# Loads in paced halves and quarters, and a new order at both ends of attention, in a one-core attention and expert-routing kernel

## The chip, the cores and the metric

The kernel runs on one core of a Trainium2 chip. The metric is the time of one execution on the device, in microseconds (us), as the median of several runs. A profile is one further execution, with its own time; its span runs from the first to the last instruction of the program.

## What is computed

Eight batches of eight heads, 576 tokens, 64 features a head, all in float32. For each head the product of k transposed and v (64 by 64) is applied to q, and each token's 64 outputs are normalised by their root mean square. The 4608 tokens, each now 512 wide, then go through one of eight experts, the one whose logit is largest.

```python
kv = np.einsum('bhsd,bhse->bhde', k, v)
out = np.einsum('bhsd,bhde->bhse', q, kv)
rms = np.sqrt(np.mean(out * out, axis=-1, keepdims=True) + 1e-06)
x = out / rms * g_norm                      # (B, S, H * D) -> (4608, 512)
logits = x @ w_gate                         # (4608, 8)
expert_idx = np.argmax(logits, axis=1)
gate_w = softmax(logits)[expert_idx]
for e in range(8):                          # D = 512, F = 1024
    h = np.maximum(x[mask_e] @ w1[e], 0.0)
    out[mask_e] = gate_w[mask_e, None] * (h @ w2[e])
```

## The kernel before

**Two stages.** Attention runs over 36 slots of 128 tokens, and sends each token's normalised row, in float16, to a table in HBM (`xs_scratch`) with a part for each expert. Then the experts run one after the other: each fetches 608 rows of its part through a transposing DMA, multiplies them with w1 (`block`, L680), applies relu on ScalarE, multiplies with w2 (`two`, L704) and scatters the gated result to the output. Rows over 608 go to a left-over job and a loop that is seldom entered.

**Order.** The order on every engine is written out by hand (`manual_schedule`, L773); each engine runs its own instructions in program order and waits for the others through semaphores. A slot `s` of the loop at L901 issues, in this order: `x_mm(s)`, q times kv with the gate's columns attached, into the PSUM tile `op` (two buffers); what the list `mid` holds for this slot; `x_qt(s + 2)`, the transposes of q on TensorE, into `qtp` (one buffer); `x_norm(s)`, the squares on ScalarE and their sum on VectorE; the list `pre`; `x_qs(s + 2)`, ScalarE's copy of the transposed q; `x_qp(s + 3)`, GpSimd's reordering copy of the loaded q; the list `late`; `rest()`, which is Ln and Exp on ScalarE, the scaled gate columns (`lr`, L354) and the scaled rows (`xh`, L359) on VectorE; and the list `last`.

The lists carry the products of k and v of the next batch (`kv_mm`, four pieces a batch, into the tile `kvp`), the copy from `kvp` (`kv_copy`), the transposes of kv and their copy (`kv_t`, `kv_tcopy`), the product with the gate weights (`kv_gate`, `kv_gcopy`), and the steps of routing a group of 2 to 5 slots (`Route`): logits, largest logit, choice, running counts, ranks on TensorE (`ranks`, L430), row numbers, and one scatter a slot on GpSimd (`scatter`, L464). `early_count` and `early_close` fix how many rows of expert 0 lie below 384 before the last groups are routed, so that its first 384 rows can be fetched, and multiplied with w1 (`early_pair`, L696), while the last slots are still routed. `zeros` issues matmuls on a tile of zeros.

**Loads.** SyncE issues all large loads in program order, on one hardware queue that is spread over 16 DMA engines. A load of k, v or q of one batch is 1152 KB, of one weight matrix 2048 KB, each one DMA (L204, L156, L162); only k and v of batch 0 come in two halves. They land in ten places of `land`, and the first five weight loads go into places of `land` that attention has left. `blank_rows` (L218) writes 128 rows a expert of a zero row with gate sum 1 into `xs_scratch`. `load_next` issues the next weight load.

Of the kernel before, what the change touches and what calls it, by code (L numbers as in the profile page):

```python
# [28 lines left out]
def kernel(  # L29
# [11 lines left out]
    nc = tc.nc  # L41
# [54 lines left out]
    c_f16 = nc.inline_tensor(c16, name="c_f16")  # L96

# [50 lines left out]

    class Weights:
# [4 lines left out]
        def load1(self, buf, eng):  # L154
            self.s1 = buf.rearrange("p (t f) -> p t f", t=4)
            eng.dma_start(  # L156
                self.s1, moe_w1[self.e, :, :].rearrange("o (t p) f -> p (o t) f", p=128)
            )

        def load2(self, buf, eng):  # L160
            self.s2 = buf.rearrange("p (t d) -> p t d", t=8)
            eng.dma_start(  # L162
                buf.rearrange("p (t c) -> p t c", t=4),
                moe_w2[self.e, :, :].rearrange("o (t p r) d -> p (o t) (r d)", p=128, r=2),
            )
# [22 lines left out]
    def load_next(count=1):  # L188
        nonlocal n_loads
        for _ in range(count):  # L190
            if n_loads < len(loads):
                n, m = loads[n_loads]
                (W[n].load1 if m == 1 else W[n].load2)(stg[n_loads % 5], nc.sync)
                n_loads += 1
# [3 lines left out]
    def load(name, b, parts=1):  # L198
        src = {"k": k, "v": v, "q": q}[name]
        n = {"k": (2 * b) % 6, "v": (2 * b + 1) % 6, "q": 6 + b % 4}[name]  # L200
        ld[name, b] = land[:, n, :].rearrange("p (i c) -> p i c", i=4)
        view = src[b].rearrange("(i hh) (p j) d -> (hh p) i (j d)", hh=2, j=9)
        return [
            lambda ii=slice(4 // parts * m, 4 // parts * (m + 1)): nc.sync.dma_start(  # L204
                ld[name, b][:, ii, :], view[:, ii, :]
            )
            for m in range(parts)
        ]
# [9 lines left out]
    def blank_rows():  # L218
        nc.sync.dma_start(
            xs.ap().rearrange("(e s) c -> s e c", e=E)[CAP - 128:CAP, :, :],  # L220
            _bc(blank, 1, E),
        )
        nc.sync.dma_start(
            xs.ap().rearrange("(e s) c -> s e c", e=E)[CAP:CAP + 32, :, 256:258],
            _bc(blank[0:32, 256:258], 1, E),
        )
# [87 lines left out]

    def x_mm(s):
        P, r, b = split(s)
        if r < 8:
            parts = [(slice(0, 128), kvs_bufs[b % 4])]
        else:
            parts = [(HALF[tok], kvs_bufs[(2 * P + tok) % 4]) for tok in range(2)]  # L320
        ops[s] = PSA.tile([128, 4, 256], F32, tag="op", bufs=2, name="op")
        for i4 in range(4):
            for cols, kvs in parts:
                nc.tensor.matmul(  # L324
                    ops[s][cols, i4, 0:144], qts[s][:, i4, cols], kvs[:, i4, :],
                    start=True, stop=True,
                )

    def x_norm(s):
# [18 lines left out]
        def rest():  # L348
# [9 lines left out]
            )  # L358
            nc.vector.tensor_tensor(  # L359
# [3 lines left out]
            )  # L363
        return rest
# [4 lines left out]
    class Route:  # L369
# [60 lines left out]
        def ranks(self, s=None):  # L430
            G = self.G
            if s is None:
                self.pp = PSA.tile([128, G, 8], F32, tag="misc", bufs=1, name="pp")
            else:
                self.pp = ops[s][:, 0, 144:144 + 8 * G].rearrange("p (t e) -> p t e", e=8)
# [182 lines left out]
    class Job:  # L618
# [84 lines left out]

        def two(self, t, yp=None):  # L704
# [69 lines left out]
    with tc.tile_pool(name="psattn", bufs=1, space=bass.MemoryType.PSUM) as PSA:  # L774
        first_slot = [9 * (b // 2) + 4 * (b % 2) for b in range(B)]
        mid, pre, late, last = ({s: [] for s in range(-4, 40)} for _ in range(4))
# [4 lines left out]
        for b in range(1, B):  # L781
            f = first_slot[b]
            for m, piece in enumerate(KV_PIECES):
                at(late, 1 + m // 2 if b == 1 else f - 5 + (m + 1) // 2 if b < 4 else f - 6 + m,
                   kv_mm, b, *piece)
            at(last, f - 2 if b == 1 else f - 3, kv_copy, b)
            at(mid, f - 1 if b == 1 else f - 2, kv_t, b)
            at(pre, f - 1 if b == 1 else f - 2, kv_tcopy, b)
            at(late if b == 1 else mid, f - 1, kv_gate, b)
            at(late if b == 1 else pre, f - 1, kv_gcopy, b)  # L790
# [5 lines left out]
            ((2, 0, 5), (23, 24, 25, 26), (26, 27, 28, 29, 29)),  # L796
            ((2, 5, 4), (27, 28, 29, 30), (30, 30, 31, 31)),
            ((3, 0, 4), (31, 32, 32, 33), (33, 33, 34, 34)),
        ]
        for g, (s_sum, s_below, s_oh, s_rank), s_scat in plan:  # L800
            rt, G = Route(*g), g[2]
            at(late, s_sum, rt.logits, 0, G)
            at(late, s_below - (s_below == s_oh), rt.top)
# [6 lines left out]
            at(mid, s_rank, rt.ranks, s_rank)  # L810
# [12 lines left out]
        at(last, 25, load_next, 1)  # L823
        at(last, 29, load_next, 1)
        ecp = []
        at(mid, 31, lambda: ecp.append(early_count()))
        at(late, 31, lambda: early_close(ecp[0]))
        at(last, 31, jobs[0].fetch, 0, NE)
        at(last, 32, load_next, 1)
        for m, slot in enumerate((31, 32, 33, 34, 34)):  # L830
            at(last, slot, W[0].cast1_act, m)
# [3 lines left out]
        at(late, 34, rt.below)  # L835
        at(late, 34, rt.code)

# [26 lines left out]
        def zeros(count, tag="misc", bufs=1):  # L864
            warm = PSA.tile([128, 4, 256], F32, tag=tag, bufs=bufs, name="warm") \
                if tag == "op" else PSA.tile([128, 2, 256], F32, tag=tag, bufs=bufs, name="warm")
            warm = warm[:, 0:2, :].rearrange("p a c -> p (a c)")

            def more(count):
                for n in range(count):  # L870
                    nc.tensor.matmul(
                        warm, blank[:, 0:64].bitcast(F16), blank[:, 0:256].bitcast(F16),
                        start=True, stop=True,
                    )
            more(count)
            return more
# [15 lines left out]
        more(1)  # L892
        kv_gate(0)
        kv_gcopy(0)
        x_qt(0)
        x_qs(0)
        x_qt(1)
        x_qs(1)
        at(late, 0, zeros, 4)

        for s in range(35):  # L901
# [3 lines left out]
            if s + 2 < 36:  # L905
                x_qt(s + 2)
# [3 lines left out]
            if s + 2 < 36:  # L910
                x_qs(s + 2)
            if s + 3 < 36:
                x_qp(s + 3)
            for fn in late[s]:
                fn()
            rest()
# [7 lines left out]
        relu = [job.early_pair(0, "kvp", 1)]  # L924
        rt.first()
        rt.choose()
        rt.tally()
        rt.ranks()
        relu.append(job.early_pair(2, "op", 2))
        W[0].cast1_act(5)  # L930
        rt.expo()
# [3 lines left out]
        rest()  # L935
        relu[0]()
        W[0].cast1_act(6)
        rt.total()
# [5 lines left out]
        W[0].cast1_act(7)  # L944
# [4 lines left out]
        relu[1]()  # L949
        end.ranks()  # L950
# [4 lines left out]
        W[0].cast2(0)  # L955
        job.early_pair(4, "kvp", 1)()
# [3 lines left out]
        job.early_pair(6, "op", 2)()  # L960
        for t in range(1, 4):
            W[0].cast2(t, nc.vector)
# [6 lines left out]
        W[1].cast1(3)  # L969
        W[1].cast2(3)  # L970

# [3 lines left out]
    if True:  # L975
        jobs[1].fetch()
        load_next(2)
        jobs[0].place(NE, CT)

        for n in range(len(order)):  # L980
# [11 lines left out]
            spans = job.spans if n > 0 else [(EARLY, CAP)]  # L992
# [71 lines left out]
```

## Time and profile before

| what | value |
|---|---|
| time, median of 3 runs | 271.45 us (271.18 to 273.37) |
| time of the profiled execution | 271.81 us, span 269.9 us |
| granted TensorE clock, mean | 0.982 |
| PE busy | 242.6 us (90% of the span) |
| ACT, DVE, POOL busy | 158.6, 142.6, 107.0 us |
| DMA | 82.93 MB, mean 307 GB/s |
| x_mm(0), x_mm(4), x_mm(35) start | 18.68, 32.91, 117.07 us |
| expert 0's first matmul, the second expert's first | 118.95, 141.37 us |

PE is TensorE, PEld its weight loads, DVE is VectorE, ACT ScalarE, POOL GpSimd, SP SyncE. In a timeline a row gives the start in us, the length in us, the engine, the line of the kernel, the operation, what it writes and reads, how many instructions it stands for, and in brackets how long the engine was idle before and what ended that. "issue" is a wait that no semaphore in the profile ended.

### The profile page before, as it was taken

What the parts mean: (1) busy time and instruction counts of PE and PEld (TensorE: products, weight loads), DVE (VectorE), ACT (ScalarE), POOL (GpSimd) and SP (SyncE); (2) the same over time, 40 slices, a digit from 0 to 9 for tenths busy, and PEclk for the clock granted to TensorE, in tenths of its full rate; (3) what the DMA queues carried; (4) which work ended last, traced back from release to release, by engine and by line L of the source; (5) the groups of instructions that cost most, each with busy time, mean ns of one, the idle gap of its engine ahead of it and who ended that gap; (6) DMA issues with size and microseconds to landing.
All of it is one profiled execution on the core that took longest, in us unless ns stands there. A gap on an engine that the chain in (4) does not pass through costs nothing. (4 is left out here: it accounts for less than half of the span.)

```text
span 269.9 us, 6884 instructions
## 1 busy us (share of the span) xinstructions
PE 242.6 (90%) x2705; PEld 171.3 (63%) x2705; DVE 142.6 (53%) x373; ACT 158.6 (59%) x363; POOL 107.0 (40%) x138
## 2 busy tenths in 40 slices
PE   4879699998999978657799999989999999999992
PEld 1658688887888867544377566465574755747740
DVE  0004367787687757987838990462524525333031
ACT  1046567676677658787547738369285692854800
POOL 8032221487278364756521061511504415042142
PEclk9789999999999999999999999999999999999997
DMA  7999999999999999579499999999999999942023
GB/s 231 340 390 393 389 352 336 392 398 400 396 383 404 417 407 352 227 174 351 106 229 410 274 307 417 256 401 359 329 419 321 369 329 313 292 126 100 16 79 109
DMA packets 53010, 82.93 MB, mean 307 GB/s; under 512 B 27747, under 2 KB 29027, under 8 KB 52976
## 3 DMA queue, kind: packets, MB, share of 16 engines
q1 hardware_dynamic: 47472, 67.95, 75.9%
q0 software_dynamic: 5056, 14.26, 14.2%
q10 hardware_dynamic: 448, 0.26, 0.6%
q8 instruction: 22, 0.36, 0.5%
q14 instruction: 12, 0.10, 0.1%
HBM read 62.31 MB, written 16.04 MB: 290 GB/s over the span
## 5 line engine op out<-in xcount | busy, mean ns | idle before, releaser
L694 ACT ACTIVATE xh<-hp 128x304 f16<-128x304 f32 (+2 forms) x128 | 52.2, 411 | 49.6 <-PE hp L682 39.9
L717 POOL DMA_INDIRECT out_dram<-ys,idx x41 | 40.9, 999 | 95.2 <-DVE ys L714 86.3
L709 PE MATMUL yp<-w2b,xh 128*128 128x512 f16 (+1 forms) x304 | 67.1, 379 | 0.0
L682 PE MATMUL hp<-xt,w1b 128*128 128x304 f16 (+2 forms) x512 | 64.4, 286 | 2.1 <-DMA xt<-xs_scratch 2.1
L682 PEld LDWEIGHTS <-w1b 128*128 128x128 f16 x544 | 51.5, 98 | 20.5 <-DMA xt<-xs_scratch 1.7
L714 DVE TENSOR_SCALAR ys<-yp,gate 128x512 f32<-128x512 f32 (+1 forms) x38 | 28.2, 749 | 67.8 <-PE yp L709 67.8
L709 PEld LDWEIGHTS <-xh 128*128 128x128 f16 (+1 forms) x328 | 33.6, 103 | 36.4 <-issue 1.2
L324 PE MATMUL op<-kvs,qts 128*128 128x144 f32 (+1 forms) x320 | 45.2, 300 | 2.6 <-DVE xh L359 1.6
L467 POOL DMA_INDIRECT xs_scratch<-xh,sli x36 | 35.8, 995 | 27.5 <-DVE xh L459 10.4
L324 PEld LDWEIGHTS op<-kvs,qts 128*128 128x128 f32 (+1 forms) x320 | 37.9, 183 | 5.7 <-ACT w1b L174 1.4
L346 DVE TENSOR_REDUCE ms<-sq 128x8 f32<-128x512 f32 x36 | 24.7, 685 | 28.9 <-ACT sq L342 28.4
L342 ACT ACTIVATE sq<-op 128x512 f32<-128x512 f32 x36 | 21.5, 596 | 20.6 <-PE op L324 14.1
L239 PE MATMUL kvp<-land 64*64 64x64 f32 x1152 | 24.7, 229 | 6.4 <-issue 3.4
L297 POOL COPY qp<-land 128x512 f32<-128x512 f32 x32 | 19.5, 616 | 24.1 <-DMA land<-in_q_dram 14.4
L239 PEld LDWEIGHTS kvp<-land 64*64 64x64 f32 x1152 | 20.6, 139 | 12.0 <-issue 12.0
L179 ACT CAST w2b<-land 128x1024 f16<-128x1024 f32 x29 | 28.1, 1042 | 0.0
L359 DVE TENSOR_TENSOR xh<-op,rinv 128x512 f16<-128x512 f32 x36 | 24.5, 679 | 0.0
L307 PE MATMUL qtp<-cf,qp 128*128 128x128 f32 x144 | 22.7, 282 | 1.7 <-POOL qp L297 1.7
L313 ACT COPY qts<-qtp 128x512 f32<-128x512 f32 x36 | 21.0, 584 | 2.2 <-PE qtp L307 1.9
L168 DVE TENSOR_SCALAR w1b<-land,g 128x1024 f16<-128x1024 f32 x28 | 19.6, 753 | 0.0
L307 PEld LDWEIGHTS qtp<-cf,qp 128*128 128x128 f32 x144 | 17.3, 146 | 2.1 <-POOL qp L297 1.1
L350 ACT ACTIVATE lnt<-ms,epsb 128x8 f32<-128x8 f32 x36 | 10.8, 300 | 6.1 <-DVE ms L346 6.0
(129 smaller groups left out, 151.3 us busy)
## 6 DMA issues: line engine op xcount, KB each, us to landing
land<-in_moe_w_dram SPq DMA_DIRECT2D x16, 2048.0 KB, 11.7
land<-in_q_dram SPq DMA_DIRECT2D x8, 1152.0 KB, 15.3
land<-in_k_dram SPq DMA_DIRECT2D x7, 1152.0 KB, 15.0
land<-in_v_dram SPq DMA_DIRECT2D x7, 1152.0 KB, 17.7
land<-in_k_dram SPq DMA_DIRECT2D x2, 576.0 KB, 6.5
land<-in_v_dram SPq DMA_DIRECT2D x2, 576.0 KB
xs_scratch<-blank SPq DMA_DIRECT2D x1, 1032.0 KB, 17.0
out_dram<-ys,idx POOLq DMA_INDIRECT x41, 6.2
```

What stands on the lines that cost most here:

```text
L179: nc.scalar.copy(self.w2[:, part, :], self.s2[:, part, :])
L239: nc.tensor.matmul(kvst[b][HALF[ipar], hh, Dh * ip:Dh * ip + Dh], kb[HALF[hh], i, cols], vb[HALF[hh], i, cols], start=(j == 0), stop=(j == 8),
L307: nc.tensor.transpose(qtps[s][:, ip, :, tok, :], qps[s][:, tok, 2 * ip:2 * ip + 2, :], ident)
L324: nc.tensor.matmul(ops[s][cols, i4, 0:144], qts[s][:, i4, cols], kvs[:, i4, :], start=True, stop=True,)
L346: nc.vector.reduce_sum(ms, sq, axis=AXX)
L359: nc.vector.tensor_tensor(xg[:, r, 0:512].rearrange("p (i c n) -> p c i n", i=2, c=4), oc[:, :, 0:128].rearrange("p c (i n) -> p c i n", i=2),
L467: go = nc.gpsimd.indirect_dma_start(out=xs_views[9 * self.P + g0 + t], out_offset=IndirectOffsetOnAxis(ap=self.sli[:, t:t + 1], axis=0), i ...
L682: nc.tensor.matmul(hp, self.w.w1[:, 2 * (kk % 2) + kk // 2, f // 2 * 256:f // 2 * 256 + 256] .rearrange("p (m r) -> p r m", r=2)[:, f % 2, :],
L694: nc.scalar.activation(self.ht[:, f, c0:c1], hp, ACTF.Relu)
L709: nc.tensor.matmul(yp[0:m, :], self.ht[:, f, t * 128:t * 128 + m], self.w.w2[:, f, :], start=(f == 0), stop=(f == 7),)
L714: nc.vector.tensor_scalar(ys[0:m, :], yp[0:m, :], self.gate[0:m, t:t + 1], None, op0=ALU.mult)
L717: nc.gpsimd.indirect_dma_start(out=self.views[t], out_offset=IndirectOffsetOnAxis(ap=self.idx[0:m, t:t + 1], axis=0), in_=ys[0:m, :], in_o ...
```

## The change

- Every load of q, k and v is now two DMAs of 576 KB, and each of the first five weight loads is four of 512 KB. Each of them is passed to `paced`, which counts 32 descriptors a load and DMA engine and makes the DMA wait on the landing of an earlier one, so that at most 48 are under way. Later weight loads are whole and not paced.
- The blank rows are copied from a constant in HBM, four rows to a piece, and not from a tile in SBUF.
- At the start, `x_qt(0)` and `x_qs(0)` come before `kv_gate(0)`; `more(1)` and the four `zeros` of slot 0 are gone. The last two pieces of `kv_mm(1)` move to `mid` of slot 2, its copy follows there, and its transposes and gate product go into slot 3 between `x_qt(4)` and `x_qt(5)`, which are both issued there.
- For batches 2 to 7, `kv_t` and `kv_tcopy` move from `mid` and `pre` to a new list `head`, behind `x_qs` and `x_qp`.
- `rest` is split: from slot 31 on, the Ln, Exp, `lr` and rows of a slot are issued in the next slot (`held`). Slots 32 and 35 use the tile `kvp` in the place of `op`.
- The routing of the groups (2,5,4) and (3,0,4) moves one slot earlier, `early_count`, `early_close` and the fetch of expert 0's first rows from slot 31 to 30; the choice of the group (3,4,3) moves from behind `x_mm(35)` into slot 34.
- Casts of the first expert's weights: of w1 on ScalarE from slot 29 on, one a slot, and of w2 on VectorE in slots 29 and 30. Two `zeros` are added in each of the slots 31 to 34.
- Behind slot 34 the early products of expert 0 begin with two single ones in the tiles `qtp` and `misc`; the steps of the last two groups are interleaved anew; and expert 0's remaining columns (384 to 608) are multiplied in pairs (`late_pair`) with one relu a pair, still in attention's PSUM pool.

```diff
+    zr = np.zeros((32, 4, RW // 2), np.float32)
+    zr[:, :, RW // 2 - 1] = 1.0
+    c_zero = nc.inline_tensor(zr.reshape(32, 2 * RW).view(np.int32), name="c_zero")
...
+    sent, PACE = [], 48
+
+    def paced(did, count):
+        room = PACE - count
+        for name, n in reversed(sent):
+            room -= n
+            if room < 0:
+                tc.add_manual_dep(
+                    did.ins, name,
+                    mybir.DependencyInfo(
+                        mybir.DependencyClass.Sync, mybir.DependencyReason.DATA
+                    ),
+                    reason="few descriptors wait in the queues at a time",
+                )
+                break
+        sent.append((did.ins.name, count))
...
-        def load1(self, buf, eng):
+        def load1(self, buf, eng, parts=1):
...
+            for m in range(parts):
+                t = slice(4 // parts * m, 4 // parts * (m + 1))
+                did = eng.dma_start(self.s1[:, t, :], view[:, t, :])
+                if parts > 1:
+                    paced(did, 32 // parts)
...
-    def load(name, b, parts=1):
+    def load(name, b, parts=2):
...
-            xs.ap().rearrange("(e s) c -> s e c", e=E)[CAP - 128:CAP, :, :],
-            _bc(blank, 1, E),
+            xs.ap().rearrange("(e s) c -> e s c", e=E)[:, CAP - 128:CAP, :].rearrange(
+                "e (p r) c -> e p (r c)", r=4
+            ),
+            _bc(c_zero.ap(), 0, E),
...
-        ops[s] = PSA.tile([128, 4, 256], F32, tag="op", bufs=2, name="op")
+        ops[s] = quad("kvp" if s in (32, 35) else "op", "op")
...
+        def late_pair(self, f, tag):
...
+            for n in range(2):
+                self.block(hp[:, n, 0:CAP - EARLY], f + n, EARLY, CAP)
+            nc.scalar.activation(
+                self.ht[:, f:f + 2, EARLY:CAP], hp[:, :, 0:CAP - EARLY], ACTF.Relu,
+            )
...
-            at(mid, f - 1 if b == 1 else f - 2, kv_t, b)
-            at(pre, f - 1 if b == 1 else f - 2, kv_tcopy, b)
-            at(late if b == 1 else mid, f - 1, kv_gate, b)
-            at(late if b == 1 else pre, f - 1, kv_gcopy, b)
+            at(head, f - 2, kv_t, b)
+            at(head, f - 2, kv_tcopy, b)
+            at(mid, f - 1, kv_gate, b)
+            at(pre, f - 1, kv_gcopy, b)
...
-            ((2, 0, 5), (23, 24, 25, 26), (26, 27, 28, 29, 29)),
-            ((2, 5, 4), (27, 28, 29, 30), (30, 30, 31, 31)),
-            ((3, 0, 4), (31, 32, 32, 33), (33, 33, 34, 34)),
+            ((2, 0, 5), (23, 24, 25, 26), (26, 27, 28, 28, 29)),
+            ((2, 5, 4), (27, 28, 28, 29), (29, 29, 30, 30)),
+            ((3, 0, 4), (31, 31, 31, 32), (32, 33, 33, 34)),
...
+        for m in range(6):
+            at(last if m < 2 else late, 29 + m, W[0].cast1_act, m)
+        for m in range(2):
+            at(late, 29 + m, W[0].cast2, m, nc.vector)
+        for n in range(31, 35):
+            at(late, n, zeros, 2)
...
-        at(late, 0, zeros, 4)
...
-            if s + 2 < 36:
+            if s < 2 or 3 < s < 34:
                 x_qt(s + 2)
             rest = x_norm(s)
             for fn in pre[s]:
                 fn()
+            put = held() if held else None
+            if put and s < 34:
+                put()
...
+            if s == 2:
+                kv_copy(1)
+            if s == 3:
+                kv_t(1)
+                kv_tcopy(1)
+                x_qt(4)
+                x_qs(4)
+                kv_gate(1)
+                kv_gcopy(1)
+                x_qt(5)
+                x_qs(5)
...
-            rest()
+            if s < 31:
+                rest()()
+            else:
+                held = rest
+                if s == 34:
+                    put()
...
-        relu = [job.early_pair(0, "kvp", 1)]
-        rt.first()
-        rt.choose()
-        rt.tally()
-        rt.ranks()
-        relu.append(job.early_pair(2, "op", 2))
+        relu = [job.early_one(0, "qtp"), job.early_one(1, "misc")]
+        rt.ranks(34)
         rt.mask()
         rt.send()
         rt.scatter(0, 3)
...
+        jobs[1].fetch()
+        load_next(2)
+        for n, tag in enumerate(("kvp", "op", "op", "misc")):
+            job.late_pair(2 * n, tag)
         W[1].cast2(3)
+        job.place(NE, CT)
```

## The prediction

> **What bounds the kernel now.** I read the slices first, then the waits of the start, then the timeline slot by slot, then the DMA issues, then the hand-over from attention to the experts.
>
> ```profile
> PE   4879699998999978657799999989999999999992
> ...
> PEclk9789999999999999999999999999999999999997
> DMA  7999999999999999579499999999999999942023
> ```
>
> TensorE fills nearly every slice of 6.75 us. Two places are thin: the first three slices, and slices 16 to 20 (108 to 135 us), where attention ends. After 135 us the experts run on a full TensorE, and the change leaves their instructions alone; so whatever is won must be won before 135 us, and it goes to the end of the span one to one. The DMA row is full too up to 108 us, so a faster start can run into the loads.
>
> ```profile
> 14.40:18.00 3.60, 2.27 (x26) 1.68 (x27) 0.00 (x0) 1.54 (x5) 2.34 (x4) 0.97 1.05 391
> 18.00:21.40 3.40, 3.40 (x17) 3.38 (x17) 0.00 (x0) 1.14 (x2) 0.00 (x0) 0.53 1.05 392
> ```
>
> These are stretches of the start: length, busy us of PE, PEld, DVE, ACT, POOL, then granted clock, DMA share, GB/s. After 3.6 us in which PE was busy for 2.27 (63%), the clock was 0.53.
>
> ```profile
> 21.33 1.03 PE L871 MATMUL warm<-blank 128*128 128x512 f16 x4
> ...
> 28.78 0.69 PE L239 MATMUL kvp<-land 64*64 64x64 f32 x29 [1.34 <-issue]
> ...
> 32.91 1.25 PE L324 MATMUL op<-kvs,qts 128*128 128x144 f32 x8 [0.47 <-ACT kvs L278]
> ...
> 35.26 1.25 PE L324 MATMUL op<-kvs,qts 128*128 128x144 f32 x8
> ...
> 53.12 0.66 PE L259 MATMUL kvtp<-cf,kvs 128*128 128x128 f32 x4 [0.38 <-ACT kvs L250]
> ```
>
> In the timeline of PE: four filler matmuls; a pause of 1.34 us in the middle of a k-by-v product, ended by no semaphore (two more like it, 0.71 us at 62.54 and 1.35 us at 96.70; each ends about 1.5 us after a 16 KB instruction packet that took 1.0 to 1.1 us, so I read them as PE waiting for instructions); and 0.38 us before the transposes of kv, once for each of the batches 2 to 7. x_mm(4) starts at 32.91, x_mm(5) at 35.26.
>
> ```profile
> 117.07 1.20 PE L324 MATMUL op<-kvs,qts 128*64 128x144 f32 x16 [1.19 <-DVE xh L359]
> ...
> 122.50 0.97 POOL L467 DMA_INDIRECT xs_scratch<-xh,sli  x1 [1.00 <-DVE lr L354]
> ...
> 127.59 1.39 POOL L467 DMA_INDIRECT xs_scratch<-xh,sli  x1 [0.30 <-issue]
> ...
> 131.05 1.23 SPq L638 DMA_TRANSPOSE xt<-xs_scratch  x1
> ...
> 134.81 3.24 PE L682 MATMUL hp<-xt,w1b 128*128 128x224 f16 x32 [1.24 <-DMA xt<-xs_scratch]
> ```
>
> The hand-over: x_mm(35), the five last scatters back to back on POOL, the fetch of expert 0's remaining rows as soon as the last scatter has landed (130.96), and the matmuls on them 3.76 us after it is issued. The next expert's rows are fetched behind it and land at 141.32, when PE comes to them (141.37). So the landing of the last scatter sets the rest.
>
> **The start.** Up to kv_t(0), which ends at 15.14, PE's order is the same. Then, with the durations above: x_qt(0) follows POOL's first copy (14.77 + 0.57), 15.40 to 16.05; kv_gate(0) 16.05 to 16.70; ACT copies qts(0) 16.10 to 16.70; x_qt(1) 16.75 to 17.40; x_mm(0) starts at 17.40 instead of 18.68. PE is then busy for about 2.9 of the 3.4 us before 17.8 where it was busy for 2.1, so I take full clock: x_mm(0) 1.25 us instead of 2.13, x_qt(2) 0.60 instead of 0.90. The four fillers (1.03) are gone. x_mm(1) at 19.25, x_qt(3) to 21.1, half of kv(1) 1.28 to 22.4, x_mm(2) to 23.6, the other half to 24.9, x_mm(3) to 26.1, kv_t(1) to 26.75, x_qt(4) to 27.35, then PE waits for ACT's copy of kvt (26.8 to 27.4), kv_gate(1) to 28.05, x_qt(5) to 28.65, x_mm(4) at 28.65, and with x_qt(6) and a piece of kv(2) x_mm(5) at 31.2: 4.1 us earlier than 35.26. The pause of 1.34 is not in this sum; without it the new order alone is worth **2.7**. The data are there: v1 landed at 21.59 and q1 at 24.58, and x_qp(4) ends at 25.35. If the clock stays low once more, 0.9 of it is lost: ends 1.8 and 2.7.
>
> **The loads.** A load in whole or in halves moves the same packets, 2304 bytes at 94 ns on one of 16 DMA engines, 32 an engine for 1152 KB. What is new is the wait: with 48 allowed and halves of 16, a half waits until the third before it has landed, and two halves (32 x 94 ns = 3.0 us) are then still queued.
>
> ```profile
> 9.00:12.00 3.00, 3.00 (x32) 1.38 (x24) 0.24 (x1) 0.00 (x0) 0.00 (x0) 0.67 1.04 411
> ...
> land<-in_k_dram SPq DMA_DIRECT2D x2, 576.0 KB, 6.5
> ...
> land<-in_v_dram SPq DMA_DIRECT2D x7, 1152.0 KB, 17.7
> ```
>
> From 9 to 12 us the queue holds halves, and moves 411 GB/s. The first load was issued at 0.73 and its first packet ran at 2.07: 1.34 us. The last semaphore packet of it ran at 4.81, the landing is 5.21: 0.4 us. So the loop from landing to new packets is 1.34 + 0.4, below 3.0, and I cost the wait at nothing; its cover is those two halves. Other end: a half that takes 4.48 us from issue to landing (the very first, 0.73 to 5.21), three in flight, gives 1.49 us a half, just the 590 KB at 395 GB/s; all beyond 4.48 is lost on every half (a rival below). Queued behind a waiting load on SP is only the next load, and from slot 30 expert 0's fetch; that one comes after load 3, whose last quarter waits for a quarter of w1 of expert 1 (whole at 106.4 before), and the fetch was issued at 115.18. Nothing waits.
>
> The Trainium skill speaks against the halves: the page "DMA: Bandwidth & Descriptors", section "Bandwidth", wants at least 1 MiB in a DMA for 75% of the peak and measured 341 GB/s at 1 MB for single ones. By it 28.3 MB of q, k, v would take at least 83 us where the kernel took some 72 and v7 would land about 11 us later; the row of 411 GB/s decides, since other halves are queued behind each.
>
> The shorter queue may shorten the three pauses (3.40 us together). Ends 0 and 3.4. A scatter issued at 47.04 into full queues had its first packet at 51.45, one issued at 111.11 into nearly empty ones at 112.67: 2.9 us are queueing, about 31 packets of 94 ns. The queue now holds 32 to 48, hardly less than that, and weights (160 ns a packet) as before; so I take **1.0**.
>
> Zero rows: 64 packets of 1032 bytes an engine at 62 ns (4.0 us) become 16 of 4128; the scatters' 4128-byte packets take 165 ns, 2.6 us if they spread over 16 engines. The loads behind come 1.4 us earlier, or, if only eight engines share them, 5.3 us and 1.3 later. The same page, section "Why a DMA increments its semaphore by 16 and not by 1", says that the outermost dimension sets how many engines work, here 8; nothing in this trace shows it, and by it slot 12 waits some 1.5 us. I take no stall: at slot 12 kv(4) starts at 56.66, v4 landed at 53.45, its first half some 1.5 earlier, which leaves room for 4.7.
>
> **Slots 5 to 28.** kv_t moves behind x_qt, so the copy from kvp is over when PE comes to it: six waits of 0.38, 2.3 in all. Ends 0 (x_mm(s+1) needs the rows of s-1 from DVE, in slot 11 done 0.8 before PE needs them) and 2.3; I take **1.5**.
>
> **Slots 29 to 34** took 15.5 us from x_mm(29) to x_mm(35), 2.6 each. Per slot now: PE 1.25 + 0.60 + two fillers 0.43 = 2.3; ACT 0.60 + 0.59 + 0.51 + a cast 0.71 = 2.4; DVE 0.69 + 0.22 + 0.68 and the routing, with the two casts of w2 (0.67 each) moved in from the tail: 3.0, 2.9, 2.5, 2.3, 1.6, 3.2. Rows written a slot later take DVE off x_mm's way, the casts put it back on: ends +1 and -1.5, I take **-0.5**. POOL: three scatters at 1.28 in slot 29 push x_qp(34) to 0.5 us behind its need, less than the 0.89 seen at 111.00.
>
> **The tail**, counted from x_mm(34) (114.64). DVE chooses for the last-but-one group before x_mm(35)'s sum of squares; its scatters start at 6.5 (7.9 before), the end group's second at 11.9 (12.95). The landing, and with it the fetch, comes **1.05** earlier; ends 0 and 1.5. PE has finished the early work at about 17.0 and idles 2.1 us until 19.1, where it idled 1.24. After a stretch 63% busy the clock fell; windows 0.56 busy at 113 and 120 us did not drop it. Ends 0 and -1.7 (3.4 us at half clock); I take **-0.3**.
>
> **Sum.** 2.7 + 1.0 + 1.5 - 0.5 + 1.05 - 0.3 = 5.45. The profiled execution took 271.81 (span 269.9 and 1.9 around it): 266.4. The median shown is 0.36 lower: **266.0**. By the worst ends 1.8 - 1.3 - 1.5 - 1.7 = -2.7, that is 274; by the best 2.7 + 3.4 + 2.3 + 1 + 1.5 = 10.9, but v4 caps what slot 12 may gain at 4.7 to 6.1, so 262.5.
>
> **Rivals.**
> The queue's pauses stay (the wait doesn't empty the queues enough): 1.0 less, 267.0, and counted with the forecast. For it: 48 is more than the 31 packets of queueing.
> The gain is given back at the hand-over and the loads: low clock at 18 and again before the late matmuls, eight engines for the zero rows, DVE the bound in slots 29 to 31. About 1.8 + 1.0 - 1.3 + 0 - 1 = 0.5 to 2.5 left: **270**. For it: DVE at 3.0 a slot. Against: each is a separate event.
> The wait starves the loads: slower. If issue to landing, with three halves in flight, takes 5.5 us, a half costs 1.83 instead of 1.49; over 44 halves v7 lands 15 us later (101 instead of 86.4) where its product in slot 25 ran at 91.56: some 10 us slower, **281**. It decides from about 1.60 us a half (4.8 us), 0.3 above the first half's. For it: that small distance. Against: that first half shared its engines with the constants; 3.0 against 1.74 us.
>
> **Chances.** Forecast with its neighbour 0.70, the gain given back 0.16, starved 0.11, above 262.5's gain 0.03. Differences under 1% (2.7 us) can't be told from none here. Faster 0.71, within 1% 0.15, slower 0.14. Range 262.5 to 271.5: it reaches through most of the given-back case and leaves out the starved one.
>
> **What would show it.** Right: x_mm(5) near 31 to 32.5 and granted clock 1.0 from 18 us; v7 landing at 85 to 87; no wait on land in slots 5 to 28; the kv_t waits of 0.38 gone; x_mm(35) to last scatter's issue about 10 us; the experts unchanged at about 128 us from the second expert on. Wrong: SP landings that stretch while GB/s falls under 390, POOL or PE waiting for land, DVE or POOL before x_mm in slots 29 to 34.

## The result, and the profile after

The change makes the kernel slower: 288.72 us (median of 4 runs, 285.81 to 290.8) against 271.69 us before (271.18 to 273.37), a ratio of 1.0536 with a 95% interval of 1.0477 to 1.0594. The profiled execution took 287.17 us, with a span of 285.4 and a mean granted clock of 0.959 (0.982 before). I had forecast 266.0 and a range of 262.5 to 271.5. Some executions are slower at a lower clock, whatever the kernel; the ratios leave them out, and one comparison below has none for that reason and was run again.

First the slices of the changed kernel, 40 of 7.1 us:

```profile
PE   5997988579898897650978999999999999999992
...
PEclk9998999979997999995799999999999999999997
DMA  7999989799999999999549999999999999943022
GB/s 236 329 325 308 295 273 344 263 348 355 339 313 294 358 323 407 409 376 230 208 139 258 403 247 370 356 277 408 298 380 365 345 413 241 356 112 131 13 75 103
```

The second half is as full as before. New are a dip of PE in slice 8, an empty slice 19 (128 to 135 us), and, all through the first 100 us, a GB/s row of 263 to 358 from the third slice on, where the kernel before had 336 to 417. The DMA row hardly shows it, with 8 or 9 in nearly every slice.

The next view gives stretches of time (length; busy us of PE, PEld, DVE, ACT, POOL; granted clock, DMA share, GB/s). Before:

```profile
16.00:32.00 16.00, 13.60 (x231) 12.13 (x229) 5.21 (x10) 8.45 (x21) 3.93 (x9) 0.89 1.05 391
40.00:62.00 22.00, 20.88 (x418) 18.12 (x409) 17.27 (x46) 16.09 (x45) 11.49 (x17) 1.00 1.06 373
```

After:

```profile
16.00:32.00 16.00, 14.05 (x243) 12.74 (x242) 5.12 (x10) 9.56 (x25) 3.74 (x9) 0.89 0.93 307
40.00:62.00 22.00, 15.33 (x303) 13.43 (x304) 12.72 (x36) 12.03 (x35) 9.80 (x14) 0.97 0.88 302
...
124.00:135.00 11.00, 1.39 (x18) 1.05 (x17) 3.66 (x12) 3.83 (x12) 2.91 (x3) 0.72 1.10 286
```

Up to 32 us PE does more than before although the loads run at 307 GB/s instead of 391: attention lives on what the first loads brought. From 40 to 62 us PE loses 5.6 us, and from 124 to 135 us it does nearly nothing, while the loads move 286 GB/s. The DMA share falls less than the bytes: of the 2304-byte packets between 16 and 32 us, most take 93 to 95 ns in both traces, but 98 of 2115 take over 200 ns (449 on average), where it was 6 of 2702; they count as busy. Of these packets 16.6 are under way at a time before, on average, and never under 15.6 over half a microsecond; after, it is 14.6, and ten of the 32 half microseconds lie between 10.8 and 14. So at times some of the 16 engines have no packet while others still work. The waits of the changed kernel say for what (us in total, times, longest):

```profile
POOL qp L329 <- DMA land<-in_q_dram: 29.3, 6, 9.5
...
PE hpe L725 <- DMA xt<-xs_scratch: 9.8, 1, 9.8
...
PE kvp L271 <- DMA land<-in_v_dram: 7.6, 6, 2.5
```

Before, PE waited for a load of v once, 2.9 us at the very start; now six times. The path, by the starts of a few steps in each trace (us):

| step | before | after | difference |
|---|---|---|---|
| x_mm(5) | 35.26 | 33.54 | -1.7 |
| x_mm(12) | 54.05 | 56.30 | +2.3 |
| x_mm(29) | 101.56 | 107.78 | +6.2 |
| x_mm(35) | 117.07 | 124.19 | +7.1 |
| first matmul of expert 0 | 118.95 | 135.15 | +16.2 |
| first matmul of the second expert | 141.37 | 157.56 | +16.2 |
| end of the span | 269.9 | 285.4 | +15.5 |

So 1.7 us are won at the start, 8.8 lost while attention waits for data, and another 9.1 at the hand-over. There the timelines of PE and of the DMA queue on SP showed before

```profile
115.18 1.39 SPq L638 DMA_TRANSPOSE xt<-xs_scratch  x1
...
118.95 1.46 PE L682 MATMUL hpe<-xt,w1b 128*128 128x384 f16 x8 [0.68 <-DMA xt<-xs_scratch]
```

and show after, PE first

```profile
124.19 1.20 PE L362 MATMUL op<-kvs,qts 128*64 128x144 f32 x16
135.15 2.72 PE L725 MATMUL hpe<-xt,w1b 128*128 128x384 f16 x8 [9.76 <-DMA xt<-xs_scratch]
```

and then SP's queue

```profile
118.27 2.84 SPq L191 DMA_DIRECT2D land<-in_moe_w_dram  x3
124.14 3.71 SPq L681 DMA_TRANSPOSE xt<-xs_scratch  x1
...
128.60 2.80 SPq L179 DMA_DIRECT2D land<-in_moe_w_dram  x4
```

The weights come behind the late q, k, v; the fetch of expert 0's first rows is issued 3.0 us after the last of their quarters that stand before it (121.10), into queues that still hold weights, with four more quarters behind it at 128.60, and PE can start 11.0 us after its issue. Before, it was issued at 115.18 into queues that had emptied at 112.28, and PE started 3.8 us later.

### The profile page after: what moved, and what is told of

Read it like the earlier page. It is cut to its first block, busy times and chain, and to the rows that moved or that the text cites. A ratio compares the mean times of both kernels' runs of the same rounds, so it can differ in the third digit from the quotient of the medians.

```text
span 285.4 us, 6945 instructions
## 1 busy us (share of the span) xinstructions
PE 247.1 (87%) x2708; PEld 175.0 (61%) x2708; DVE 142.3 (50%) x374; ACT 155.9 (55%) x359; POOL 106.9 (37%) x138
## 5 line engine op out<-in xcount | busy, mean ns | idle before, releaser
L737 ACT ACTIVATE xh<-hp 128x304 f16<-128x304 f32 (+1 forms) x120 | 49.2, 413 | 44.8 <-PE hp L725 31.8
L725 PEld LDWEIGHTS <-w1b 128*128 128x128 f16 x544 | 52.3, 99 | 30.6 <-issue 14.2
L725 PE MATMUL hp<-xt,w1b 128*128 128x304 f16 (+1 forms) x480 | 61.1, 288 | 0.0
L362 PE MATMUL op<-kvs,qts 128*128 128x144 f32 (+1 forms) x320 | 46.9, 307 | 0.4 <-DVE xh L400 0.4
L362 PEld LDWEIGHTS op<-kvs,qts 128*128 128x128 f32 (+1 forms) x320 | 39.7, 189 | 3.5 <-DVE xh L400 0.7
L207 ACT CAST w2b<-land 128x1024 f16<-128x1024 f32 x28 | 27.2, 1043 | 0.0
L725 PE MATMUL hpe<-xt,w1b 128*128 128x384 f16 x32 | 7.4, 397 | 9.8 <-DMA xt<-xs_scratch 9.8
## 6 DMA issues: line engine op xcount, KB each, us to landing
land<-in_moe_w_dram SPq DMA_DIRECT2D x11, 2048.0 KB, 13.8
```

Source lines behind the costliest of these rows:

```text
L207: nc.scalar.copy(self.w2[:, part, :], self.s2[:, part, :])
L362: nc.tensor.matmul(ops[s][cols, i4, 0:144], qts[s][:, i4, cols], kvs[:, i4, :], start=True, stop=True,)
L725: nc.tensor.matmul(hp, self.w.w1[:, 2 * (kk % 2) + kk // 2, f // 2 * 256:f // 2 * 256 + 256] .rearrange("p (m r) -> p r m", r=2)[:, f % 2, :],
L737: nc.scalar.activation(self.ht[:, f, c0:c1], hp, ACTF.Relu)
```

## The experiments

Theory 1: the wait starves the load stream. A cover of two halves (32 descriptors, 3.0 us) is shorter than the time from a landing to the next data. Theory 2: the new zero rows, on few DMA engines, cost the time. Theory 3: the new order costs it. The runs were made on four chips, on which the kernel before took 271.2 to 275.3 us (medians). A ratio compares executions on one chip; the start of a step is compared with the one trace of before, so that differences of a microsecond or two between two traces carry little.

### The change without its wait

```diff
-    sent, PACE = [], 48
+    sent, PACE = [], 100000
```

> The changed kernel with the number of descriptors allowed under way raised out of reach, so that no load waits for another; halves, quarters, zero rows and order stay. Theory 1 (the wait ties the 16 DMA engines together: the loads fell from 385 to 308 GB/s between 12 and 40 us, and the late weights then delay the fetch at the hand-over): 268 to 272 us, 380 GB/s or more from 12 to 40 us, x_mm(35) before 115 instead of 124.2, the wait on xt of 9.8 us below 2. Theory 2 (the zero rows, now 44032-byte packets, cost the 8 us that slots 11 to 13 lost): about 280 us. Theory 3 (the new order is slow by itself at the hand-over): 280 us or more, with the wait on xt still there.

Measured: 0.9933 of the kernel before (0.9897 to 0.9969), 272.86 against 275.25 us on the same chip. The waits take all of the loss with them, and from 16 to 32 us the loads are back at 390 GB/s:

```profile
16.00:32.00 16.00, 12.58 (x244) 11.41 (x243) 5.06 (x11) 9.32 (x25) 4.35 (x10) 1.00 1.05 390
```

This version is faster than both kernels, than the one before by 0.7%, with an interval clear of 1.

### The wait alone, on the kernel before

The loads in halves, the first weights in quarters and the wait at 48, with order and zero rows as before (`paced`, `load1`, `load2`, `load` and `load_next` from the change, nothing else).

> The kernel before with halves, quarters and the waits alone; order and zero rows as before. Theory 1: 279 to 287 us, loads near 310 GB/s between 12 and 40 us. Theories 2 and 3: 270 to 273 us.

Measured: 1.0377 (1.0305 to 1.0448). In the stretch of 16 to 32 us:

```profile
16.00:32.00 16.00, 14.29 (x241) 12.22 (x240) 5.21 (x10) 9.31 (x23) 3.90 (x9) 0.89 0.95 319
```

The hand-over's loss is here too: x_mm(35) at 122.20 (+5.1), expert 0 at 132.70 (+13.8). Theory 1 holds, and theory 3 is not needed for it. But the wait costs 3.8% here and about 6% in the changed kernel (1.0536 against 0.9933); what the rest of the change adds to it was not separated.

### Old zero rows, with the wait

```diff
-            xs.ap().rearrange("(e s) c -> e s c", e=E)[:, CAP - 128:CAP, :].rearrange(
-                "e (p r) c -> e p (r c)", r=4
-            ),
-            _bc(c_zero.ap(), 0, E),
+            xs.ap().rearrange("(e s) c -> s e c", e=E)[CAP - 128:CAP, :, :],
+            _bc(blank, 1, E),
```

> The changed kernel with the zero rows written as before, from SBUF in 1032-byte packets; the waits stay. Theory 1: 279 to 284 us, slots 11 to 13 get some 5 of their 8 us back, the loads stay near 310 GB/s. Theory 2: 276 to 279 us. Theory 3: 287 us, no difference beyond 2 us.

Measured: 288.02 us (281.14 to 290.31), without a ratio. So it was run once more:

> The changed kernel with its wait at 48, and the zero rows of the kernel before. If the zero rows cost under the wait what the stall at slots 11 to 13 of the changed kernel looks like, some 5 us come back: 283.5, 1.043. If the stream's rate alone sets the end (the data are late anyway, and what the zero rows delay is made up), nothing comes back: 288, 1.055 to 1.065.

Measured: 1.0468 (1.0421 to 1.0514); the intervals of this and of the changed kernel (1.0477 to 1.0594) overlap. The ratio is nearer to the first of the two expectations than to the second. Its waits:

```profile
POOL qp L327 <- DMA land<-in_q_dram: 23.6, 5, 10.3
...
PE kvp L269 <- DMA land<-in_v_dram: 6.5, 4, 2.7
```

With the old rows x_mm(12) starts at 55.03 and x_mm(13) at 61.10, with the new ones 56.30 and 61.77: most of the stall that I had put down to the new rows is there without them: from x_mm(11) to x_mm(13) it is 9.5 us, 11.0 with the new rows, 5.9 in the kernel before. The old rows are a megabyte in the same place of the queue. Theory 2 falls as the cause, since 4.7% are lost without the new rows and nothing is lost with them where nothing waits; a price of the new rows under the wait, 0.7% by the two ratios, is not settled.

### Order and sizes, with neither wait nor new zero rows

> The changed kernel without the waits and with the zero rows as before: what is left is the new order, the halves and the quarters. Theory 1 and 2: 265 to 269 us, as forecast, x_mm(5) at 31 to 32.5, x_mm(35) near 112. Theory 3: over 272 us.

Measured: 0.996 (0.9917 to 1.0003), 274.17 against 275.25. On the scale of the first comparison (271.69) that is 270.6, between the two expectations: the order does not lose, and it does not win what I had forecast for it. With the run without the wait (0.9933) it bounds the zero rows in a full queue: nothing that can be told from none.

### How long the queue must be

The wait alone, on the kernel before, with other limits:

```diff
-    sent, PACE = [], 48
+    sent, PACE = [], 64
```

> As the run of the wait alone (the kernel before with halves, quarters and waits), with 64 descriptors allowed instead of 48: one more half, 1.5 us more of work, in the queue. With 48, 1.77 MB were under way at a time and 316 GB/s came out from 12 to 40 us, which is a loop of 5.6 us. Theory 1a (the loop is a fixed latency of about 5.6 us): 64 restores 385 GB/s and 270 to 274 us relative to 271.5 before. Theory 1b (the loop is long because a landing waits for the slowest of 16 engines, whose lag grows with what is under way): 64 gives 335 to 365 GB/s and a time halfway, 274 to 280.

> The same with 96 allowed, three loads under way. Theory 1a: 385 GB/s, within 1% of before. Theory 1b: 370 to 385 GB/s, within 2% of before.

Measured: 0.9975 (0.9925 to 1.0025) with 64, 0.9993 (0.9923 to 1.0063) with 96. The stretch with 64:

```profile
16.00:32.00 16.00, 14.19 (x241) 12.19 (x239) 5.21 (x10) 9.04 (x24) 4.12 (x9) 0.89 1.05 380
```

One half more under way and the loss is gone, which is what 1a expected (385 GB/s, here 379 from 12 to 40 us) and not 1b. In this stretch a half is issued every 1.49 us (19.94, 21.44, 22.93, 24.41) and the first three land 5.94 us after their issue: that is four times 1.49, the rate of the engines. Whether the loop really is the fixed 5.6 us of 1a, the run with one half at a time tells: it is not.

### Which loads

The wait at 48 on q, k, v alone, and on the quarters of the weights alone:

> The kernel before with halves and quarters, the wait at 48 on the loads of q, k and v alone; the weight quarters don't wait. If the loss is the late stream of q, k, v and what follows from it (late slots, weights that meet the fetch of expert 0): 3 to 4% slower, as with the wait on all. If the waits of the weight quarters, which sit on SyncE ahead of that fetch, make a good part: under 2% slower.

> The counterpart: the wait at 48 on the weight quarters alone, the halves of q, k and v don't wait. First case: within 1% of before. Second case: 2% slower or more.

Measured: 1.035 (1.0315 to 1.0385) on q, k, v, 1.0016 (0.9969 to 1.0063) on the weights. The hand-over loses as much where the weights don't wait (x_mm(35) at 119.20, expert 0 at 129.97, where 1.9 us lay between them before and 10.8 do now): the weights are late because they stand behind late q, k, v, not because of their own wait.

### One half at a time

The limit at 16 on q, k, v, so that each half waits for the landing of the one before; the weights don't wait.

> The kernel before with halves, quarters and the wait on q, k and v at 16 descriptors: the next half is issued only when the one before has landed, so that the time from issue to landing of a lone half is measured. My forecast's terms (1.34 to the first packet, 0.4 after the last one, 1.5 for the packets) give 3.2 to 3.4 us, some 175 GB/s from 12 to 40 us. The run with 48 needs more: at least 4.5 us, 130 GB/s or less, that is a fixed part of 3.0 or more. The time itself says nothing here (over 300 us).

Measured: 375.14 us in one execution, 149 GB/s from 12 to 40 us, between the two expectations. The issues of SP's queue, where a row of x2 is two halves:

```profile
20.76 0.37 SPq L228 DMA_DIRECT2D land<-in_q_dram  x1
24.45 3.97 SPq L228 DMA_DIRECT2D land<-in_k_dram  x2
31.79 4.01 SPq L228 DMA_DIRECT2D land<-in_v_dram  x2
...
40.41 4.11 SPq L228 DMA_DIRECT2D land<-in_q_dram  x2
```

A lone half lands 3.7 us (k, median) to 3.9 us (v) after its issue, and the next is issued 0.02 us after the landing. Of 3.7 us, 1.49 is the time of its own packets at full rate; the loop that the cover has to hide is 2.2 us, not the 1.74 I had added up, but still below 3.0. So a lone transfer does not explain the loss. The trace also tells where my 1.74 went wrong: the first packet of a half runs 1.01 us after its issue and the next issue comes 0.38 us after the last packet (medians of 43 halves), together 1.39, less than my 1.34 + 0.4. But from the first packet to the end of the last it is 2.41 us and not 1.49: the engines, with 16 packets each, do not start and end together, and some packets take over 200 ns (54 of 1024 from 16 to 32 us). In a busy stream the engines are further apart. By the landing events the 16 engines finish a lone half within 0.6 us of each other (median), a half of the changed kernel within 1.9 us, 4.9 at most. A half has landed only when the slowest engine is through; the others, some 1.3 us further ahead than in the lone case, have used up that much of their cover.

### The same limit in smaller pieces

To tell that from a cost of the waiting itself: q, k, v in quarters (`parts=4` in `load`), same limit of 48. Each load now waits twice as often, but 40 descriptors are left when the next quarter is released.

> The kernel before with its order and zero rows, q, k, v in quarters (8 descriptors an engine) and the weights in quarters, all waiting at the same 48. A quarter then waits for the sixth before it, and five quarters, 40 descriptors or 3.8 us, cover the loop where two halves covered 3.0. Theory 1: the slack over the lone half's 2.2 us grows from 0.8 to 1.6 us, so most of the loss of the wait alone (1.038) goes: 345 to 380 GB/s from 12 to 40 us and a ratio of 1.00 to 1.02. Rival: what costs is the waiting itself (each wait of SP holds the stream up), and with twice as many waits it is as slow or slower: 1.038 or more.

Measured: 1.0056 (1.0012 to 1.01). From 16 to 32 us:

```profile
16.00:32.00 16.00, 13.77 (x234) 12.35 (x235) 5.21 (x10) 8.54 (x21) 3.53 (x8) 0.89 1.01 368
```

From 12 to 40 us the mean is 335, a little below what I expected, with a weak stretch around 34 us (262 GB/s from 32 to 36); but most of the time is back, with more waits at the same limit. The rival falls. Packets under way are 15.8 at a time on average, 15.0 with the wait alone in halves and 16.5 with 64.

| limit | left when the next is released | GB/s, 16 to 32 us | time |
|---|---|---|---|
| 16, halves | 0 | 148 | 1.38 (one execution) |
| 48, halves | 32 descriptors, 3.0 us | 319 | 1.0377 |
| 48, quarters | 40, 3.8 us | 368 | 1.0056 |
| 64, halves | 48, 4.5 us | 380 | 0.9975 |
| 96, halves | 80, 7.5 us | 390 | 0.9993 |
| none, whole | - | 391 | 1 |

(All on the order of the kernel before. In the first row the weights don't wait, in the others they wait too. The 94 ns a descriptor are those of the prediction.) Lone loop 2.2 plus 1.3 us of lag is 3.5 us, and the rate does recover between 3.0 and 3.8 to 4.5. That a cover of 3.0 us is too short, and one of 4.5 is enough, is shown by these runs. That the lag is what eats the cover is argued from the numbers above; no run changed the lag by itself.

### The changed kernel with 64

> The changed kernel whole, with 64 descriptors allowed in place of 48. Theory 1 (the cover of two halves is too short, 3.0 us against 2.2 us of a lone half plus the lag of the engines behind each other): with three halves covering (4.5 us) the loads run at 375 GB/s or more from 12 to 40 us and the time is that of the change without a wait, 0.993 of the kernel before, within 0.987 and 1.000. Theory 2 (the new zero rows on eight engines cost much under any wait): slots 11 to 13 still lose 3 us or more and the ratio is above 1.01.

Measured: 0.9938 (0.9894 to 0.9981), 384 GB/s from 12 to 40 us; as good as without a wait, and with the new zero rows. So no cost of these shows here, and the wait itself can stay if it is loose enough; no gain from it shows either.

### The parts of the order

The new start (with kv_t behind x_qt) on the kernel before, loads whole; the new hand-over alone (everything that changes from slot 27 on, halves, no wait); and the start with the new zero rows. The run of the hand-over holds one move that the list of the change leaves out: a weight load goes from slot 25 to slot 27.

> The kernel before with whole loads, and of the change only the new order of the start (slots 0 to 3) and kv_t behind x_qt. Theory A (the start and kv_t gain what the forecast said, 2.7 + 1.5, and the hand-over gives it back): 1.0 to 1.6% faster than before, x_mm(29) 3.5 to 4.5 us earlier, from x_mm(29) to the second expert's first matmul 39.8 us as before. Theory B (the start's gain is eaten by the longer pause of PE in the first product of batch 1, 2.4 to 2.7 us where it was 1.34): within 0.5% of before, x_mm(29) at most 1.5 us earlier.

> The changed kernel without the waits, with the zero rows as before and with start and kv_t as before: the new order from slot 27 on is what is left, with loads in halves and quarters. Theory A: 0.7 to 1.2% slower than before, 42 to 43 us from x_mm(29) to the second expert's first matmul (39.8 before, 42.7 in both runs without the wait). Theory B: within 0.5% of before, 40 us.

> The start and kv_t, whole loads without waits, and the zero rows from HBM. It would be faster than both kernels if theory A holds. With the 44032-byte packets on eight engines in a deep queue: like the run of the start alone, within 0.4%; if they delay k4 and v4 by more than 1.5 us, slower than it by 1 to 2 us.

Measured: 0.9976 (0.9942 to 1.0009) for the start, 1.0048 (1.0013 to 1.0083) for the hand-over, 0.997 (0.9939 to 1.0002) for the start with the zero rows. Theory B fits better: both lie within 0.5%, and the hand-over alone takes 40.4 us from x_mm(29) to the second expert, not the 42.7 of the two runs without the wait (what they lose there stands below, under the tail and the clock). Why the start gives so little is in PE's timeline of the last:

```profile
21.79 1.28 PE L244 MATMUL kvp<-land 64*64 64x64 f32 x72 [1.60 <-DMA land<-in_v_dram]
...
27.96 0.73 PE L244 MATMUL kvp<-land 64*64 64x64 f32 x20 [2.75 <-issue]
28.62 2.29 PE L329 MATMUL op<-kvs,qts 128*128 128x144 f32 x8
...
35.89 0.88 PE L329 MATMUL op<-kvs,qts 128*128 128x144 f32 x5
```

x_mm(0) starts 1.6 us earlier than before, then v of batch 1, in one piece, is late by 1.60; then comes the pause in the product of batch 1 that no semaphore ends, 2.75 us instead of 1.34; and behind it the granted clock is half, so that x_mm(3) takes 2.29 instead of 1.25. x_mm(5) is no earlier. The same pause in the changed kernel without its wait:

```profile
26.50 0.56 PE L271 MATMUL kvp<-land 64*64 64x64 f32 x20 [2.70 <-issue]
...
33.09 1.25 PE L362 MATMUL op<-kvs,qts 128*128 128x144 f32 x8
```

There v1 comes in halves in time, the clock stays up, and 2.2 us of the lead survive to x_mm(5). That is the best of the eight traces with the new start: in them x_mm(0) comes between 16.9 and 18.6, and x_mm(5) between 33.1 and 36.5.

## Why the prediction was wrong

**The step that failed** is "So the loop from landing to new packets is 1.34 + 0.4, below 3.0, and I cost the wait at nothing". The sum was 5.45 us of gain; without the wait the same kernel gains 0.7%, some 1.8 us; with it the kernel loses 5.4%. So the wait costs about 6%, 16 us, and it stood in the sum as 0, at both ends of the range too. Two things were wrong in it. The loop was mis-sized: measured, it is 2.2 us for a lone half. The two pieces that I had added up came to 1.39 us and not 1.74; what I left out, that the packets of a half are not through in 1.49 us, is 0.9 us for a lone half. In a busy stream the engines drift apart (in the trace of before, where I could have seen it, the 16 engines finish a load within 2.35 us of each other, median), and as far as is argued above that lag brings the loop to some 3.5 us, past the cover of 3.0. And the comparison left no room for either: 3.0 against 1.74 looked like nearly double.

**The rival "the wait starves the loads"** had the mechanism right, and its arithmetic was good where it went: from issue to landing of 5.5 us it put the landing of v7 at 101; measured are 5.3, 6.4 and 6.2 us (medians for k, v, q), and v7 landed at 100.7. That the two agree so well is partly luck: by the same arithmetic the measured 6.0 us or so would have given 109.

```profile
land<-in_k_dram SPq DMA_DIRECT2D x16, 576.0 KB, 5.3
land<-in_v_dram SPq DMA_DIRECT2D x16, 576.0 KB, 6.4
land<-in_q_dram SPq DMA_DIRECT2D x16, 576.0 KB, 6.2
```

Its point of decision, 4.8 us, was passed. Its price, 281, was too low by nearly 8 because it stopped at the products of v: x_mm(35) is 7.1 us late (some 10 forecast), but the loads of the weights and the fetch behind them lose 9.1 more at the hand-over. "Nothing waits", of what is queued behind a waiting load on SP, was the second wrong sentence; I had tested it with the old times of the stream. And 0.11 was too small a chance for a rival that was decided by 0.3 us of an operation the trace of before didn't show.

**The start** (2.7, the pause apart): x_mm(0) was forecast for 17.40 and came at 17.42 without the wait and 17.70 with it, and at full clock as forecast (1.15 and 1.25 us). But x_mm(5) came at 33.09 and 33.54, not 31 to 32.5. What is late next is PE's own pause, 1.34 us before: 2.70 us without the wait, 1.51 with it and half clock behind it (x_mm(3) 2.17 us). I had taken the pause as a length that stays or shrinks; with the new start it was 1.51 to 3.08 us in the eight traces, with the old one from nothing to 1.51. PE comes to it some 3 us earlier (at 23.6 to 25.2 instead of 26.9 to 28.4), but it ends less than 2 us earlier (25.7 to 28.0 instead of 27.8 to 29.5), so it takes back a good part of the lead. In the start run alone (0.9976) the gain can't be told from none.

**Shorter pauses** (1.0): not so. The pause at the start grew. In the changed kernel those near 62 and 97 us are gone, but PE is late there and waits for data; without the wait none over 0.33 us is left there either, and one of 1.51 us is back at 96.89 in that of order and sizes without wait. They come and go between executions, and a shorter queue is not what removes them.

**Waits for the copy from kvp** (1.5): in the changed kernel PE's six of 0.38 are gone, in order and sizes without wait two of up to 0.8 us are left. From x_mm(5) to x_mm(29) the trace without the wait needs 64.65 us against 66.30, that of order and sizes 66.27, that of the start with the zero rows 63.99; so 0 to 2.3. But the 66.30 hold two of the pauses above, 2.06 us together, and the other three 0.9, 2.5 and 1.4 us of such pauses; without them the gain is about 0.4 in the first two and 1.7 in the third.

**Slots 29 to 34** (-0.5): x_mm(29) to x_mm(35) takes 16.6 (no wait), 17.2 (order and sizes), 16.5 (hand-over alone) and 16.2 (with 64) for 15.5 before. The sign was right, the size 0.7 to 1.7, beyond -0.5 and up to just past my worst end of -1.5. And the tail below counts from x_mm(34), so that the two terms share the stretch from x_mm(34) to x_mm(35), which became 0.9 us shorter; up to x_mm(34) the loss is 1.6 to 2.6.

**The tail** (1.05, counted from x_mm(34)): the last scatter was forecast at 11.9 us instead of 12.95, and came at 12.0 to 12.1 in the hand-over alone, in order and sizes and with 64; without the wait at 14.0. From x_mm(34) to the second expert it is 26.7 us before; 25.4 in the hand-over alone, 27.1 in order and sizes, 27.6 without the wait. So from 1.3 won to 0.9 lost. Behind the scatters, from the first late product to the second expert, it is 7.3 us (at full clock) where it was 6.6, 0.63 of it a wait of PE for the relu of a pair, which I had not counted. And in the trace without the wait:

```profile
117.80 2.72 PE L725 MATMUL hpe<-xt,w1b 128*128 128x384 f16 x8 [2.23 <-DMA xt<-xs_scratch]
120.31 0.23 PE L480 MATMUL op<-csum,ch 128*128 128x24 f16 x1
```

The ranks of the last-but-one group now stand on PE behind the first two early products, and these wait 2.23 us for expert 0's rows; so that group's scatters start 8.5 us after x_mm(34) (121.39), not 6.5 as forecast, and later than the 7.9 before. I had counted VectorE's steps and not what stands ahead of the ranks on TensorE. Where the rows were there in time (the other three traces) the 6.5 came true.

That is the rival "the gain is given back at the hand-over and the loads", at 0.16: it left 0.5 to 2.5 us of gain, and the kernel without its wait shows 1.8. Of the change without its wait, it was the better forecast, but only in part for its reasons: the low clock shows, a cost of the eight engines does not.

**The clock** (-0.3): the early products and their start lie in a half-clock stretch in several of these traces (from 117.6 to 121 us without the wait; from 128.7 to 139 in the changed kernel, after 9.76 us of idle PE). The late products, which the term was about, ran at full clock without the wait (3.23 us) and at half clock in order and sizes (4.89): nothing or 1.7 lost, the two ends that I had given.

**Zero rows**: I took 2.6 us on 16 engines. The trace has 24 packets of 44,032 bytes in eight chains of three, 1.63 us each where nothing disturbs them, which reads as 4.9 us on each of eight engines (the trace gives no engine for a packet). This is what the Trainium skill's page "DMA: Bandwidth & Descriptors", section "Why a DMA increments its semaphore by 16 and not by 1", says of an outermost dimension of 8, and the end of 5.3 was the right one; in a full queue no cost of it shows (0.997 with, 0.9976 without).

**Halves**: unpaced, they move 390 GB/s from 16 to 32 us, as whole loads do (391). The row of 411 was rightly preferred to the page's rule on large transfers (section "Bandwidth"), whose table gives one time for a transfer of each size.

**The experts**: from the second expert on to the end 127.8 us, 128.5 before; forecast unchanged.

## What to carry to other kernels

A wait that limits what is under way needs a cover, at the moment it releases the next transfer, that is longer than the time of a lone transfer beyond its own packets, with room for the lag of the slowest DMA engine (that last part is argued, not shown). Here, from 16 to 32 us, a cover of 3.0 us cost a fifth of the bandwidth, 3.8 a twentieth, 4.5 almost nothing. Where such a wait is added, price it from both ends and follow a late stream to the last load behind it, the small fetch at the end of the queue too: here that was more than half of the loss. And an earlier start is worth something only if what PE needs next comes earlier as well: data, or whatever ends its pauses.

## What the runs showed that I had not expected

- The 16 DMA engines do not work on a transfer in step: landings of one 576 KB half spread over 1.9 us in the paced stream and 0.6 us for a lone one (medians).
- When the stream runs dry, the DMA share falls by 0.12 (1.05 to 0.93) and the bytes by a fifth, since a few packets take over 200 ns; GB/s is the row to read.
- The pause of PE near 26 to 29 us, which no semaphore ends, grew where PE came earlier. In all traces together there are 28 such pauses over 0.6 us between 20 and 115 us, and each ends 1.2 to 1.6 us after the end of a 16 KB instruction packet. That fits the reading of the prediction, PE waiting for instructions; no run moved these packets, so it stays unproven.
- The granted clock changes in stretches of 3.41 us. Behind that pause it fell to half in seven of the eight traces with the new start (an x_mm then took 2.1 to 2.3 us instead of 1.25), where PE had been busy for 0.19 to 0.56 of the stretch before the drop. Without the wait, after a pause of 2.70 us, it did not fall: there the pause lay in two stretches, busy for 0.52 and 0.69. So neither the length of a pause nor the busy share of one stretch decides alone.
- Zero rows written from 4128-byte pieces went as packets of 44,032 bytes, 1.63 us each.
